# The end of a fused attention and SoLU kernel: one unit's store placed earlier, and the last unit's output split over two PSUM banks in another way

## The chip, the core and the metric

The kernel runs on one core of a Trainium2 chip. TensorE (PE) multiplies matrices into PSUM, whose eight banks hold 512 float32 numbers in each of 128 partitions. VectorE (DVE), ScalarE (ACT) and GpSimd (POOL) work on tiles, and SyncE (SP) issues most of the DMA transfers. Each engine takes its own instructions in order; engines wait for each other through semaphores. The metric is the device time of one execution in microseconds (us).

## The reference

There are two stages. The first is a linear attention with a decaying state, for 4 batches, 8 heads, 768 steps and a head size of 48. The second takes the rows of the first (3,072 rows of 384) through a layer with a SoLU activation and a layer norm:

```python
for t in range(S):
    cur = np.einsum('bhd,bhe->bhde', u[None] * kt, vt)
    y[:, :, t] = np.einsum('bhd,bhde->bhe', rt, state + cur)
    state = wt[:, :, :, None] * state + np.einsum('bhd,bhe->bhde', kt, vt)
...
h = x @ w_in
e = np.exp(h - h_max)
sm = e / (np.sum(e, axis=-1, keepdims=True) + 1e-09)
solu = h * sm
ln = (solu - mu) / np.sqrt(var + 1e-06) * g_ln
return (ln @ w_out).astype(np.float32)
```

## The kernel before

The rows are cut into 24 units of 128 rows, numbered 0 to 23 (six chunks of 128 steps, each for four batches). A unit goes through the attention and then through the second stage. Only the second stage of the last four units, 20 to 23, concerns us here.

**The second stage of a unit.** `H` multiplies the transposed rows by `w_in` into PSUM, 1,024 hidden numbers for each of 128 rows. `e` is the exponential of these (ACT), `he` the product of both (DVE), `hq` the square of `he` (ACT, in one half of the last unit DVE). `Oa` and `Ob` are the two halves of the output product (PE): `he` times `w_out`, 384 columns, and in further columns the sums that the norm needs, made with `he`, `e` (or `ea`, pairs of `e` that POOL has added) and `hq`. `w_out` carries the gain and is centred beforehand, so that the mean needs no subtraction, and the norm comes to one factor for each row. That factor takes three small steps: `qm` (DVE, the variance from the sums), `lv` (ACT, logarithm), `rs` (ACT, the inverse root through the exponential). `o` multiplies the 384 columns by it (ACT, or DVE where the word ends in `.d`), and `out` stores 192 KB to memory.

Two variants matter. Units 16, 18 and 20 turn `he` by a DMA and take their sums from other instructions; their `qm` needs a step `sq` (ACT), which reads the output's sum. The last unit, 23, is cut in halves of 512 hidden numbers: `HA`, `EA`, `DA`, `QA` are product, exponential, `he` and `hq` of the first half, `HB`, `EB`, `DB`, `QB` those of the second.

**What sets the order.** The order is written out by hand, as a long string of words, `ORDER` (lines 21 to 65). A word is a step and a unit: `qm21` is the variance of unit 21, `H22.0` the hidden product of unit 22 into bank 0. The words are carried out from first to last, and class `InOrder` (line 70) keeps the instructions of each engine in that order. So moving a word moves its instruction ahead of others on its own engine and on no other. The part of the order that the change touches is lines 62 to 64:

```python
out18 HB23.4 e22 Ob20 o19.d EA23 he22 hq22.a EB23 qm21 sq20 DA23 ea22.p lv21 qm20 lv20 DB23 QB23.d rs21 Oa22.7
QA23.a rs20 out17 Ob22 qm22 o20.a out19 lv22 Oa23.6 o21.d rs22 Ob23.s34 out20 out21 o22.a qm23 lv23 rs23 out22
o23.a out23.h
```

Ahead of these stand `H22.0` and `Oa21.2 HA23.3 Ob21`, so PE makes the hidden product of unit 22, then the first half of the output of unit 21, the first half of the hidden product of unit 23, the second half of the output of unit 21, and then `HB23` and `Ob20`.

**The output of the last unit** is made by `last_output` (line 586). It has three regions in three banks: 256 columns in bank 6, the sums (three columns) in bank 3, 128 columns in bank 4. In its first half it makes two of the eight matmuls of the 256 columns and half of the sums; in its second half the other sums, the remaining six matmuls of the 256 columns, and eight of the 128 columns. `scaled_out` (line 665) scales the 256 columns on ACT and the 128 columns on DVE, and `store` (line 676) sends the first from ACT's queue and the second from SP's.

Of the kernel before, what the change touches and what calls it, by code (L numbers as in the profile page):

```python
# [8 lines left out]
F32 = mybir.dt.float32  # L9
# [5 lines left out]
COPY = mybir.ActivationFunctionType.Copy  # L15
ALU = mybir.AluOpType
MULT, ADD, SUB = ALU.mult, ALU.add, ALU.subtract
# [41 lines left out]
e20 st19 xt19 he20 H19.0 Y22.n5 Oa17.7 kt23 e19 dv23 qm16 Ob17 y22.d ht18 M23.4 xt21 he19 lv16 rs16 o16.d Oa18.3  # L59
Ob18 hq20.a H21.0 hq18.a hq19.a m23.d ht20 xt22 out14 sq18 sv20 qm18 e21 lv18 ea19.p Y23.n2 rs18 Oa19.6 qm17  # L60
ea21.p lv17 rs17 y23.d Ob19 he21 Oa20.5 hq21.a qm19 out16 H22.0 o17.d xt23 lv19 o18.d rs19 Oa21.2 HA23.3 Ob21
out18 HB23.4 e22 Ob20 o19.d EA23 he22 hq22.a EB23 qm21 sq20 DA23 ea22.p lv21 qm20 lv20 DB23 QB23.d rs21 Oa22.7
QA23.a rs20 out17 Ob22 qm22 o20.a out19 lv22 Oa23.6 o21.d rs22 Ob23.s34 out20 out21 o22.a qm23 lv23 rs23 out22
o23.a out23.h
"""

# [34 lines left out]
def kernel(  # L101
# [14 lines left out]
    C = 128  # L116
    NC = S // C
    DM = H * D
# [3 lines left out]
    KF = DF // 128  # L122
# [4 lines left out]
    NU = len(units)  # L127

    InOrder.transfer = None
    pe, act, dve, pool, sp = (InOrder(tc, e, e in (nc.scalar, nc.sync))  # L130
                              for e in (nc.tensor, nc.scalar, nc.vector, nc.gpsimd, nc.sync))
# [13 lines left out]
    def bank(shape, dtype, slot, name):  # L145
        size = 1
        for d in shape[1:]:
            size *= d
        first = int(slot) * 512
        if dtype == BF16:  # L150
            part = banks[:, first:first + size // 2].bitcast(BF16)
        else:
            part = banks[:, first:first + size]
        if len(shape) == 2:
            return part
        names = "abc"[:len(shape) - 1]
        return part.rearrange(f"p ({' '.join(names)}) -> p {' '.join(names)}", **dict(zip(names, shape[1:])))
# [35 lines left out]
    one_col = consts.tile([C, 2], BF16)  # L193
    dve.memset(one_col, 1.0)
    inv_col = consts.tile([C, 2], BF16)
# [13 lines left out]
    w2 = consts.tile([128, KF, DM + 2], BF16)  # L209
# [126 lines left out]
    live = [dict() for _ in units]  # L336
# [245 lines left out]
    ending = [word[2:].partition(".s") for word in ORDER.split() if word.startswith(f"Ob{NU - 1}.s")]  # L582
    split = bool(ending)
    DL = DM * 2 // 3

    def last_output(i, part):
        L = live[i]
        e, he, hq = e_t[i % NWK], he_t[i % NWK], hq_t[i % NWK]
        half = range(part * KF // 2, (part + 1) * KF // 2)
        first = 2  # L590
        if part == 0:
            for f in range(first):
                pe.matmul(L["o_ps"], lhsT=he[:, f, :], rhs=w2[:, f, :DL], start=(f == 0), stop=False)
            L["s_ps"] = bank([C, 3], F32, ending[0][2][0], "s_ps")
        s_ps = L["s_ps"]
        for f in half:
            pe.matmul(s_ps[:, :2], lhsT=he[:, f, :], rhs=w2[:, f, DM:], start=(f == 0), stop=False,
                      skip_group_check=True)
            pe.matmul(s_ps[:, :2], lhsT=e[:, f, :], rhs=inv_col, start=False, stop=False, skip_group_check=True)
        for f in half:  # L600
            pe.matmul(s_ps[:, 2:], lhsT=hq[:, f, :], rhs=one_col[:, :1], start=False, stop=(f == KF - 1),
                      skip_group_check=True)
        if part:
            for f in range(first, KF):
                pe.matmul(L["o_ps"], lhsT=he[:, f, :], rhs=w2[:, f, :DL], start=False, stop=(f == KF - 1))
            r_ps = L["r_ps"] = bank([C, DM - DL], F32, ending[0][2][1], "r_ps")
            for f in range(KF):
                pe.matmul(r_ps, lhsT=he[:, f, :], rhs=w2[:, f, DL:DM], start=(f == 0), stop=(f == KF - 1))

    def output(i, part):  # L610
        L = live[i]
        e, he, hq, o_ps = e_t[i % NWK], he_t[i % NWK], hq_t[i % NWK], L["o_ps"]
        if i == NU - 1 and split:
            last_output(i, part)
            return
        for f in range(part * KF // 2, (part + 1) * KF // 2):
            if i in by_rows:
                pe.matmul(o_ps[:, :DM + 1], lhsT=he[:, f, :], rhs=w2[:, f, :DM + 1], start=(f == 0), stop=(f == KF - 1))
                continue
            pe.matmul(o_ps[:, :DM + 2], lhsT=he[:, f, :], rhs=w2[:, f, :], start=(f == 0), stop=False,  # L620
                      skip_group_check=True)
            if i not in added:
                pe.matmul(o_ps[:, DM:DM + 2], lhsT=e[:, f, :], rhs=inv_col, start=False, stop=False,
                          skip_group_check=True)
            elif f % 2 == 0:
                pe.matmul(o_ps[:, DM:DM + 2], lhsT=ea_t[i % NWK][:, f // 2, :], rhs=inv_col, start=False, stop=False,
                          skip_group_check=True)
            if i not in paired:
                pe.matmul(o_ps[:, DM + 2:], lhsT=hq[:, f, :], rhs=one_col[:, :1], start=False, stop=(f == KF - 1),
                          skip_group_check=True)  # L630
            elif f % 2 == 0:
                pe.matmul(o_ps[:, DM + 2:], lhsT=hq[:, f // 2, :], rhs=one_col[:, :1], start=False,
                          stop=(f == KF - 2), skip_group_check=True)

    def output_a(i, x):
        live[i]["o_ps"] = bank([C, DL if i == NU - 1 and split else DM + 3], F32, x, "o_ps")
        output(i, 0)

    def output_b(i, x):
# [8 lines left out]
    def variance(i, x):  # L648
        if i in by_rows:
            dve.tensor_sub(out=qm_t[i % NWK], in0=s2_t[i % NWK], in1=sq_t[i % NWK][:, 0:1])  # L650
            return
        s_ps = live[i]["s_ps"] if i == NU - 1 and split else live[i]["o_ps"][:, DM:]
        dve.tensor_scalar(out=qm_t[i % NWK], in0=s_ps[:, :1], scalar1=s_ps[:, 1:2], scalar2=s_ps[:, 2:],
                          op0=MULT, op1=ADD)

# [9 lines left out]
    def scaled_out(i, x):  # L665
        o_ps, rs, o = live[i]["o_ps"], rs_t[i % NWK], o_t[i % NWK]
        if i == NU - 1 and split:
            act.activation(out=o[:, :DL], in_=o_ps, func=COPY, scale=rs)
            dve.tensor_scalar(out=o[:, DL:], in0=live[i]["r_ps"], scalar1=rs, scalar2=None, op0=MULT)
            return  # L670
        if x == "d":
            dve.tensor_scalar(out=o, in0=o_ps[:, :DM], scalar1=rs, scalar2=None, op0=MULT)
        else:
            act.activation(out=o, in_=o_ps[:, :DM], func=COPY, scale=rs)

    def store(i, x):
# [13 lines left out]
        krk=transposed_k, krr=transposed_r, kr=transposed_copy, M=scores, m=scores_copy, sel=scores_mask,  # L690
        Y=attend, y=y_copy, S=state, et=state_decay, st=state_update, X=x_transposed, xT=x_copy,
        H=hidden, e=hidden_exp, he=hidden_mul, ea=hidden_add, qa=square_add, hq=hidden_square, Oa=output_a, Ob=output_b,
        sq=sums, qm=variance, lv=scale, rs=root, o=scaled_out, out=store,
        HA=first_half[0], EA=first_half[1], DA=first_half[2], QA=first_half[3],
        HB=second_half[0], EB=second_half[1], DB=second_half[2], QB=second_half[3],
# [36 lines left out]
```

## Time and profile before

| | |
|---|---|
| runs | 142.66, 143.30 and 144.29 us |
| median | 143.3 us |
| profiled execution: its own time | 144.28 us |
| its span, first to last instruction | 142.5 us |
| granted clock of PE, mean | 0.992 |
| PE busy | 126.0 us (88% of the span) |
| DVE busy | 122.7 us (86%) |
| ACT busy | 118.6 us (83%) |
| POOL busy | 118.4 us (83%) |

The profiled execution lies at the upper end of the three runs; 1.8 us of its time lie outside the span. In a row of the timeline the first number is the start of an instruction in microseconds from the start of the span, the second how long it took; then come the engine (PEld is PE's weight load; a q behind the name is the engine's sequencer, which issues DMAs), the line, the operation and its output and input tiles with their shapes. A bracket gives the idle time of the engine ahead of the instruction, and what ended it. All instructions go through a helper, so that all have line 86, and they are told apart by tile and shape. PSUM is the tile `ps`, `w` as an input of a matmul with `he` is the output weight.

### The profile page before, as it was taken

The page shows a single profiled execution, that of the slowest core. Times are in us where ns is not written, and L with a number is a line of the kernel's source. Part 1 is how long each engine was busy: PE and PEld are TensorE (multiplying, and loading weights), DVE is VectorE, ACT ScalarE, POOL GpSimd, SP SyncE. Part 2 cuts the span into 40 slices and gives each one's busy share as a digit, 9 for nine tenths or more (in the row PEclk, how much of TensorE's full clock was granted, in tenths as well). Part 3 has the DMA queues.
Part 4 walks back from the last instruction along what each step waited for, and adds up shares of the span by engine and source line. Part 5 has one row for each costly group of instructions (what it writes and reads, how often), then busy time and mean ns, then how long its engine had stood idle before and what let it go on. Part 6 is the DMA issues. An engine that isn't in the chain of part 4 may idle for free.

```text
span 142.5 us, 4827 instructions
## 1 busy us (share of the span) xinstructions
PE 126.0 (88%) x1901; PEld 95.7 (67%) x1906; DVE 122.7 (86%) x203; ACT 118.6 (83%) x243; POOL 118.4 (83%) x152
## 2 busy tenths in 40 slices
PE   0598966968999999999969999999999999999970
PEld 0146545657967887669858797788866766787760
DVE  6147889996999999999987999899999999878760
ACT  3658799959999999999986989998677889897780
POOL 7999999979999999999999999999999693402300
PEclk9999999999999999999999999999999999999996
DMA  4999999999999999999999899999999897562314
GB/s 93 272 300 346 316 282 384 389 293 225 249 249 244 290 250 294 246 224 230 234 191 278 197 230 212 281 158 223 176 218 208 134 246 80 136 182 68 127 59 167
DMA packets 94713, 31.98 MB, mean 224 GB/s; under 512 B 88585, under 2 KB 92818, under 8 KB 94690
## 3 DMA queue, kind: packets, MB, share of 16 engines
q1 hardware_dynamic: 70578, 20.79, 67.9%
q10 hardware_dynamic: 22128, 4.79, 15.6%
q0 software_dynamic: 1984, 6.10, 14.1%
q8 instruction: 15, 0.25, 0.7%
q14 instruction: 8, 0.07, 0.1%
HBM read 22.03 MB, written 4.72 MB: 188 GB/s over the span
## 4 chain that ended last, share of the span: by engine, by line
PE 48%; DMA 16%; POOL 14%; ACT 10%; DVE 5%; issue 3%; ACTq 0%; POOLq 0%; DVEq 0%
PE ps L86 48%; DMA win_f<-in_moe_w_in_dram 5%; DMA kr<-kp 5%; DMA kr_in<-in_r_dram 4%; POOL w L86 3%; DMA xT<-y 3%; POOL q L86 2%; ACT ps L86 2%; ACT hq L86 2%; POOL win_sb L86 1%; POOL p L86 1%; ACT e L86 1%; DVE kr L86 1%; POOL dv L86 1%; DVE he L86 1%
## 5 line engine op out<-in xcount | busy, mean ns | idle before, releaser
L86 PE MATMUL ps<-w,he 128*128 128x386 bf16 (+4 forms) x208 | 43.5, 312 | 0.0
L86 PE MATMUL ps<-xT,win_sb 128*128 128x128 bf16 x504 | 31.2, 219 | 0.2 <-DVE kr L86 0.2
L86 ACT ACTIVATE e<-ps 128x1024 bf16<-128x1024 f32 (+1 forms) x25 | 24.6, 987 | 7.5 <-PE ps L86 6.6
L86 PEld LDWEIGHTS <-win_sb 128*128 128x128 bf16 x504 | 29.0, 98 | 1.8 <-DVE kr L86 0.3
L86 DVE TENSOR_TENSOR kp<-ps,kr_in 128x768 bf16<-128x768 f32 x24 | 22.6, 950 | 7.9 <-DMA kr_in<-in_r_dram 4.2
L86 DVE TENSOR_TENSOR he<-ps,e 128x1024 bf16<-128x1024 f32 (+1 forms) x22 | 25.6, 1170 | 2.2 <-ACT e L86 1.9
L86 DVE TENSOR_TENSOR m<-ps,keep 128x1024 bf16<-128x1024 f32 x22 | 26.6, 1215 | 0.8 <-PE ps L86 0.7
L86 PE MATMUL ps<-one_col,hq 128*128 128x1 bf16 x168 | 26.7, 164 | 0.0
L86 POOL TENSOR_TENSOR p<-kr_in 128x384 bf16<-128x384 f32 x24 | 23.9, 1003 | 0.3
L86 ACT ACTIVATE hq<-he 128x1024 bf16<-128x1024 bf16 (+1 forms) x21 | 21.6, 1031 | 0.7 <-DVE he L86 0.7
L86 POOL TENSOR_TENSOR dv<-vb,dg 128x384 bf16<-128x384 bf16 x24 | 19.8, 829 | 2.6 <-DVE dg L86 2.3
L86 POOL TENSOR_TENSOR q<-p,u_bc 128x384 bf16<-128x384 bf16 x24 | 21.7, 914 | 0.1
L86 PEld LDWEIGHTS <-he 128*128 128x128 bf16 x208 | 19.1, 96 | 3.5
L86 ACT ACTIVATE ps<-ps 128x768 f32<-128x768 f32 x24 | 19.0, 796 | 2.4 <-PE ps L86 2.2
L86 PEld LDWEIGHTS <-hq 128*128 128x128 bf16 x168 | 14.1, 96 | 8.3
L86 POOL TENSOR_TENSOR ea<-e 128x512 bf16<-128x512 bf16 x9 | 10.3, 1150 | 9.4 <-ACT e L86 9.4
L86 ACT ACTIVATE lw<-w_in 128x384 bf16<-128x384 f32 x24 | 12.3, 521 | 5.5 <-DMA w_in<-in_w_dram 5.5
L86 PE MATMUL ps<-inv_col,e 128*128 128x2 bf16 x96 | 15.1, 165 | 0.0
L86 PEld LDWEIGHTS <-kp 128*128 128x128 bf16 x176 | 12.2, 104 | 3.9 <-DVE kp L86 2.1
L86 PEld LDWEIGHTS <-kr 64*128 64x128 bf16 (+1 forms) x272 | 10.3, 96 | 6.1 <-issue 1.8
L86 DVE TENSOR_REDUCE dg<-q 128x8 f32<-128x384 bf16 x24 | 12.8, 542 | 0.0
L86 POOL DMA_DIRECT2D kr_in<-in_r_dram x12 | 11.0, 921 | 0.3 <-POOL p L86 0.3
(97 smaller groups left out, 271.5 us busy)
## 6 DMA issues: line engine op xcount, KB each, us to landing
out_dram<-o SPq DMA_DIRECT2D x23, 192.0 KB, 3.2
kr_in<-in_k_dram SPq DMA_DIRECT2D x13, 192.0 KB, 5.1
kr_in<-in_r_dram POOLq DMA_DIRECT2D x12, 192.0 KB, 5.1
w_in<-in_w_dram SPq DMA_DIRECT2D x11, 192.0 KB, 5.2
kr_in<-in_r_dram SPq DMA_DIRECT2D x10, 192.0 KB, 5.3
v_in<-in_v_dram SPq DMA_DIRECT2D x10, 192.0 KB, 5.5
v_in<-in_v_dram POOLq DMA_DIRECT2D x9, 192.0 KB, 4.2
w_in<-in_w_dram ACTq DMA_DIRECT2D x8, 192.0 KB, 3.6
```

Of the source, the lines that this page charges most:

```text
L86: made = make(*args, **kwargs)
```

## The change

It has two parts.

First, in the order, `qm21 lv21 rs21` move ahead of `EA23 he22`. `o21.d` moves to a place behind `DA23`. `out17`, `out19` and `out21` move ahead of `ea22.p`; among the transfers this puts `out21` ahead of `out20`, the others keep their places. On DVE the order becomes `o19, qm21, he22, DA23, o21, qm20, DB23, QB23, qm22, qm23, o23`, where it was `o19, he22, qm21, DA23, qm20, DB23, QB23, qm22, o21, qm23, o23`. On ACT it becomes `e22, lv21, rs21, EA23, hq22, EB23, sq20, lv20, QA23, rs20, o20, ...`, where it was `e22, EA23, hq22, EB23, sq20, lv21, lv20, rs21, QA23, rs20, o20, ...`. On PE and POOL no word moves.

Second, the last unit's output has two regions: 128 columns and the three sums in bank 6, and 256 columns in bank 3. The 128 columns and two of the sums are made by one matmul of 130 columns for each of the eight parts of `he`. The 256 columns come last, in eight matmuls. There are 32 matmuls where there were 40. `scaled_out` issues the DVE instruction (128 columns) ahead of the ACT instruction (256 columns).

```diff
-out18 HB23.4 e22 Ob20 o19.d EA23 he22 hq22.a EB23 qm21 sq20 DA23 ea22.p lv21 qm20 lv20 DB23 QB23.d rs21 Oa22.7
-QA23.a rs20 out17 Ob22 qm22 o20.a out19 lv22 Oa23.6 o21.d rs22 Ob23.s34 out20 out21 o22.a qm23 lv23 rs23 out22
+out18 HB23.4 e22 Ob20 o19.d qm21 lv21 rs21 EA23 he22 hq22.a EB23 sq20 DA23 out17 out19 o21.d out21 ea22.p qm20
+lv20 DB23 QB23.d Oa22.7 QA23.a rs20 Ob22 qm22 o20.a lv22 Oa23.6 rs22 Ob23.s3 out20 o22.a qm23 lv23 rs23 out22
 o23.a out23.h
...
     def last_output(i, part):
-        half = range(part * KF // 2, (part + 1) * KF // 2)
-        first = 2
-        if part == 0:
-            for f in range(first):
-                pe.matmul(L["o_ps"], lhsT=he[:, f, :], rhs=w2[:, f, :DL], start=(f == 0), stop=False)
-            L["s_ps"] = bank([C, 3], F32, ending[0][2][0], "s_ps")
-        s_ps = L["s_ps"]
-        for f in half:
-            pe.matmul(s_ps[:, :2], lhsT=he[:, f, :], rhs=w2[:, f, DM:], start=(f == 0), stop=False,
+        for f in range(part * KF // 2, (part + 1) * KF // 2):
+            pe.matmul(L["o_ps"][:, :DM - DL + 2], lhsT=he[:, f, :], rhs=w2[:, f, DL:], start=(f == 0), stop=False,
                       skip_group_check=True)
-            pe.matmul(s_ps[:, :2], lhsT=e[:, f, :], rhs=inv_col, start=False, stop=False, skip_group_check=True)
-        for f in half:
-            pe.matmul(s_ps[:, 2:], lhsT=hq[:, f, :], rhs=one_col[:, :1], start=False, stop=(f == KF - 1),
+            pe.matmul(L["o_ps"][:, DM - DL:DM - DL + 2], lhsT=e[:, f, :], rhs=inv_col, start=False, stop=False,
                       skip_group_check=True)
+        for f in range(part * KF // 2, (part + 1) * KF // 2):
+            pe.matmul(L["o_ps"][:, DM - DL + 2:], lhsT=hq[:, f, :], rhs=one_col[:, :1], start=False,
+                      stop=(f == KF - 1), skip_group_check=True)
         if part:
-            for f in range(first, KF):
-                pe.matmul(L["o_ps"], lhsT=he[:, f, :], rhs=w2[:, f, :DL], start=False, stop=(f == KF - 1))
-            r_ps = L["r_ps"] = bank([C, DM - DL], F32, ending[0][2][1], "r_ps")
+            l_ps = L["l_ps"] = bank([C, DL], F32, ending[0][2], "l_ps")
             for f in range(KF):
-                pe.matmul(r_ps, lhsT=he[:, f, :], rhs=w2[:, f, DL:DM], start=(f == 0), stop=(f == KF - 1))
+                pe.matmul(l_ps, lhsT=he[:, f, :], rhs=w2[:, f, :DL], start=(f == 0), stop=(f == KF - 1))
...
         if i == NU - 1 and split:
-            act.activation(out=o[:, :DL], in_=o_ps, func=COPY, scale=rs)
-            dve.tensor_scalar(out=o[:, DL:], in0=live[i]["r_ps"], scalar1=rs, scalar2=None, op0=MULT)
+            dve.tensor_scalar(out=o[:, DL:], in0=o_ps[:, :DM - DL], scalar1=rs, scalar2=None, op0=MULT)
+            act.activation(out=o[:, :DL], in_=live[i]["l_ps"], func=COPY, scale=rs)
             return
```

Here `DM` is 384, `DL` is 256 and `KF` is 8.

More of the change, by code (lines that the diff above doesn't have):

```diff
@@ L635, in output_a @@
     def output_a(i, x):
-        live[i]["o_ps"] = bank([C, DL if i == NU - 1 and split else DM + 3], F32, x, "o_ps")
+        live[i]["o_ps"] = bank([C, DM - DL + 3 if i == NU - 1 and split else DM + 3], F32, x, "o_ps")
         output(i, 0)
@@ L651, in variance @@
             return
-        s_ps = live[i]["s_ps"] if i == NU - 1 and split else live[i]["o_ps"][:, DM:]
+        s_ps = live[i]["o_ps"][:, -3:]
         dve.tensor_scalar(out=qm_t[i % NWK], in0=s_ps[:, :1], scalar1=s_ps[:, 1:2], scalar2=s_ps[:, 2:],
```

## The prediction

> **What bounds the kernel now.** I read the page first, then the chain of waits in order of time, then the timeline of each engine over the last 13 us, because the first word that the change moves belongs to unit 21.
>
> ```profile
> span 142.5 us, 4827 instructions
> PE 48%; DMA 16%; POOL 14%; ACT 10%; DVE 5%; issue 3%; ACTq 0%; POOLq 0%; DVEq 0%
> ```
>
> Over the whole span the chain is mostly PE, but the change works only on the end. There the chain leaves PE:
>
> ```profile
> 120.36 10.55 PE ps L86 x156
> 130.91 0.02 issue
> 130.93 1.03 ACT e L86
> ```
>
> From 130.9 on it goes through e22 on ACT, then he22 on DVE (the first row below), and then mostly along ACT. So a step put ahead of he22 on DVE is put straight into the chain, unless its data is there by 131.98. DVE's timeline:
>
> ```profile
> 131.98 1.23 DVE L86 TENSOR_TENSOR he<-ps,e 128x1024 bf16<-128x1024 f32 x1 [0.62 <-ACT e L86]
> 133.19 0.29 DVE L86 TENSOR_SCALAR qm<-ps 128x1 f32<-128x1 f32 x1
> 133.40 0.68 DVE L86 TENSOR_TENSOR he<-ps,e 128x512 bf16<-128x512 f32 x1
> 134.88 0.16 DVE L86 TENSOR_TENSOR qm<-s,sq 128x1 f32<-128x1 f32 x1 [0.80 <-ACT sq L86]
> 134.96 0.68 DVE L86 TENSOR_TENSOR he<-ps,e 128x512 bf16<-128x512 f32 x1
> 135.67 0.69 DVE L86 SCALAR_TENSOR_TENSOR hq<-he 128x512 bf16<-128x512 bf16 x1
> 136.28 0.28 DVE L86 TENSOR_SCALAR qm<-ps 128x1 f32<-128x1 f32 x1
> 136.48 0.61 DVE L86 TENSOR_SCALAR o<-ps,rs 128x384 f32<-128x384 f32 x1
> 137.01 0.28 DVE L86 TENSOR_SCALAR qm<-ps 128x1 f32<-128x1 f32 x1
> 138.13 0.35 DVE L86 TENSOR_SCALAR o<-ps,rs 128x128 f32<-128x128 f32 x1 [0.85 <-ACT rs L86]
> ```
>
> In order these are he22, qm21, DA23, qm20, DB23, QB23, qm22, o21, qm23 and o23. PE, where qm21's data comes from and where the last unit ends:
>
> ```profile
> 132.99 0.16 PE L86 MATMUL ps<-one_col,hq 128*128 128x1 bf16 x1
> 133.01 0.83 PE L86 MATMUL ps<-xT,win_sb 128*128 128x128 bf16 x12
> ...
> 136.67 0.24 PE L86 MATMUL ps<-one_col,hq 128*128 128x1 bf16 x4
> 136.77 1.27 PE L86 MATMUL ps<-w,he 128*128 128x256 bf16 x14
> ```
>
> The first row is the last matmul of Ob21 (HB23 follows it), the last two end the sums of unit 23 and its columns. ACT:
>
> ```profile
> 133.24 1.06 ACT L86 ACTIVATE hq<-he 128x1024 bf16<-128x1024 bf16 x1 [0.19 <-DVE he L86]
> 134.21 0.58 ACT L86 ACTIVATE e<-ps 128x512 bf16<-128x512 f32 x1
> ...
> 135.07 0.29 ACT L86 ACTIVATE lv<-sq,qm 128x1 f32<-128x1 f32 x1
> 135.27 0.19 ACT L86 ACTIVATE rs<-lv 128x1 f32<-128x1 f32 x1
> 135.37 0.61 ACT L86 ACTIVATE hq<-he 128x512 bf16<-128x512 bf16 x1
> 135.88 0.19 ACT L86 ACTIVATE rs<-lv 128x1 f32<-128x1 f32 x1
> 136.10 0.58 ACT L86 ACTIVATE o<-ps,rs 128x384 f32<-128x384 f32 x1
> 136.60 0.20 ACT L86 ACTIVATE lv<-qm 128x1 f32<-128x1 f32 x1
> ...
> 137.77 0.20 ACT L86 ACTIVATE rs<-lv 128x1 f32<-128x1 f32 x1
> 138.00 0.47 ACT L86 ACTIVATE o<-ps,rs 128x256 f32<-128x256 f32 x1
> 138.51 0.37 ACTq L86 DMA_DIRECT2D out_dram<-o  x1
> ```
>
> From hq22 (133.24) to the last store's issue (138.51) ACT has hardly a gap. What is late at its start is late at its end.
>
> **The change part by part.** *qm21 ahead of he22.* Nothing ahead of Ob21 changes on PE, so the sums of unit 21 end at 132.99 + 0.16 = 133.15, 1.17 after he22 could start. On DVE he22 is now queued behind qm21, and qm21 waits. It starts between 133.15 and 133.19 (where it started before, directly behind he22). The instruction behind it followed 0.21 later (133.19 to 133.40), so he22 starts at 133.36 to 133.40 for 131.98: 1.38 to 1.42 late. I take 1.42.
>
> On ACT lv21 is queued ahead of EA23 and waits for qm21 as well, until 133.5. With rs21 that makes two steps of about 0.2, and EA23 (as long as EB23, 0.58) then ends near 134.5. The next instruction, hq22, waits for he22 until 134.66 anyway (133.24 + 1.42). So the hold on EA23 costs nothing beside the hold on he22; without that cover it would cost 1.4.
>
> *How the 1.42 travels.* hq22 134.66, EB23 135.63, qm20 (which waits for sq20 behind EB23) 136.30, lv20 136.49. rs21 no longer stands between lv20 and QA23, which saves the 0.10 between the rows at 135.27 and 135.37: QA23 136.69, rs20 137.20, o20 137.42. On DVE, qm20 at 136.30 leads as before to DB23 136.38, QB23 137.09 and qm22 137.70, and qm22 ends at 137.98. lv22 waits for that, so it starts at 138.02, again 1.42 late, and the 0.10 is lost. Then rs23 139.19, o23 on ACT 139.42, its store 139.93.
>
> *o21 and out21 earlier.* o21 (0.61) leaves its place behind qm22 for one ahead of qm20, where DVE idled 0.80 for sq20: free both before and after. Its store can go near 135.9 for 137.13, one store less in the last burst. On SP it now stands ahead of out20, whose data comes at 138.0 (136.10 + 0.58 + 1.32), so it holds nothing; `ea22.p`, which the stores are moved past, is POOL's, and POOL's order stays.
>
> *The new split.* Every input of PE is at most 1.42 late. Matmuls of 128 columns follow each other in (0.83 - 0.17)/12 = 0.055 us, so the eight of 130 columns in place of eight of 2 add at most 8 x 0.055 = 0.44 ahead of the sums' end, and the two of 256 that leave that stretch take back 0.22. The sums end by 136.91 + 1.42 + 0.22 = 138.55, qm23 by about 138.9; lv23 wants it at 138.97 (0.22 ahead of rs23). The 256 columns, 8 x 0.11 = 0.88 more, are done by about 139.4, when ACT's o23 can start. So by this upper bound PE just stays out of the way, and its saving (eight matmuls of 128 columns, at most 0.44) lies beside ACT's chain. One thing is gained: o23 on DVE started at 138.13, held by PE (whose last row ends at 138.04), though rs23 was done at 137.97; now it follows rs23 at once.
>
> *The stores.*
>
> ```profile
> 136.71 0.33 SPq L86 DMA_DIRECT2D out_dram<-o  x1
> 137.13 1.50 SPq L86 DMA_DIRECT2D out_dram<-o  x1
> 139.21 0.40 SPq L86 DMA_DIRECT2D out_dram<-o  x1
> DMA to landing us min/median/max: 1.8/2.0/3.0
> q8 instruction: 1, 0.02, 13.3%
> ```
>
> These are single rows of five answers: the issues of out20, out21 and SP's part of out23 in short windows of SP's timeline, the landing times of the stores after 124, and the instruction queue within 137.0 to 137.5. SP's last store was ready at 138.13 + 0.35 = 138.48 but issued at 139.21, because out21's issue took 1.50 in place of 0.3 to 0.4 and held SP. Now DVE's o23 ends at 139.42 + 0.35 = 139.77, and SP is free if no issue is held: 139.81, 0.60 later than before. With 2.0 to land, 141.8 (ACT's 139.93 gives 141.9), against 141.2. So between 0.6 and 0.7 of the 1.42 reach the end of this execution: 144.28 + 0.65 = 144.9.
>
> The long issue stands beside a fetch of 16 KB that took 13.3% of 16 x 0.5 us, or 1.06 us of one DMA engine. The Trainium skill ("Runtime: NRT & Kernel Launch", Instruction fetch mechanics) says that a sequencer fetches its next 16 KiB block while it executes the current one, and that this is mostly hidden. By that rule the long issue is no regular part of the kernel, and its relief no gain of the change; by the row, it would be.
>
> How this stands to the median: 143.3 is 0.98 below the profiled execution. Without the long issue out22 would have gone near 137.7 and the last store at 138.52, 0.69 sooner, which leaves the profiled execution at 143.6. So the median looks like an execution without it, and there the change costs 139.81 - 138.52 = 1.29. The ends for the median are +0.6 and +1.4; I take +1.2, near the latter: 144.5.
>
> **The rivals.** *Not slower: the stores set the end, and the wait is short.* From the last result (138.48) to the end of the span 4.0 us pass. With the shortest landing (1.8), an issue at once and the 1.3 from the last landing (141.2) to the end, they could be 3.1, so a tail without held stores gives back 0.9 at most. The wait would have to be below that: Ob21 would have to end by 132.6. If qm21 found its data by 131.98, the 0.10 on ACT and the 0.16 on DVE's o23 would come off, and up to 0.7 of tail: 142.6 to 143.2. For it: SP's held store. Against it: PE has no gap from H22 to the row at 132.99. Chance 0.10. That the new order makes no difference at all (143.3): 0.04.
>
> *A held issue again.* If a fetch meets the last stores once more, out22 (ready at 139.1) is held 1.5 and SP's part of out23 goes at 140.7, 0.9 later than in my sum: 145.4. For it: that the row exists; against it: the median. Chance 0.10.
>
> *PE's clock falls in the stall.* PE now waits for hq22, at most 1.42 longer than before.
>
> ```profile
> 139.50:140.00 0.50, 0.00 (x0) 0.00 (x0) 0.00 (x0) 0.00 (x0) 0.00 (x0) 1.00 1.05 375
> 140.00:140.50 0.50, 0.00 (x0) 0.00 (x0) 0.00 (x0) 0.00 (x0) 0.00 (x0) 0.56 1.08 398
> ```
>
> The seventh number after the stretch's length, the one ahead of the DMA share, is the granted clock. PE's last matmul ended at 138.04, and until 140.0, 1.96 later, the clock was still 1.00; it fell after that. The stall is shorter, so the clock should hold. If it fell all the same, the 3.7 us of PE work from hq22's end (134.30) to 138.04 would take 3.7/0.56 = 6.6, 2.9 more, almost all of it on the end: about 147. The Trainium skill ("TensorE: Matmul & The Clock Gate", A second HAM failure mode) tells of a kernel whose clock swung because PE idled briefly and often between groups; by that rule this would happen here, but PE's clock of 1.00 after 1.96 us of rest speaks against it. Chance 0.02.
>
> **How the numbers follow.** The forecast, that he22's wait moves the chain by 1.42 and the stores give a part of it back, has 0.74, with a time of 144.5. The held issue has 0.10 (145.4), the clock 0.02 (147), the short wait with the stores 0.10 (142.6 to 143.2), no difference 0.04 (143.3). The three runs of before lie 1.6 apart, so a median of few runs can be 0.5 off; I add that to the forecast's own ends (143.9 to 144.7), and a little of the held issue's side. The range is 143.4 to 145.4, which leaves out the clock, part of the short wait and the upper end of a held issue.
>
> One per cent is 1.4 us, about what a measurement of this kernel can tell from no change. Slower by over 1% means above 144.7: a good third of the forecast (0.28), the held issue and the clock, 0.40 together. Faster by over 1% means below 141.9, under every time that I worked out; for the short wait with a lucky median I leave 0.03. Within 1% is the rest, 0.57.
>
> **What would show it.** In the profile of the changed kernel DVE's qm21 should start near 133.2 after an idle time of about 1.8, which its row gives to PE, with he22 behind it near 133.4. hq22 should start near 134.7, ACT's o23 near 139.4, and ACT should idle about 1.5 ahead of lv21. PE should have an idle time near 135 and be done before ACT's o23. DVE's o23 should start with rs23's end, no longer with PE's. SP's issues should run o21, o20, o22, o23, with the last near 139.8 and none above 0.5.
>
> The prediction is wrong if Ob21's sums come well ahead of 133.1, so that he22 starts near 132; if the last store of SP goes at 139.2 or sooner; or if something late in the chain proves to have slack, so that ACT's o23 starts less than 1.2 later while he22 started 1.4 later.

## The result, and the profile after

The changed kernel takes 144.76 us (median of four runs, 144.43 to 145.50), the kernel before beside it 143.55 us (142.66 to 144.29). The ratio is 1.0108, with a 95% interval of 1.0064 to 1.0152: 1.2 us slower. The profiled execution of the changed kernel took 145.50 us, its span 143.8 us, for 144.28 and 142.5 us before. All ratios are of fast runs alone; the profiles of four of the kernels below (the changed one with Ob21 ahead of HA23, the kernel before with 40 more instructions, the split with 60 more, the changed one with 48 more) are of slow executions, in which PE's granted clock stood at 1.00 from e22 to the end of PE's work.

DVE's timeline of the changed kernel, from o19 on, the rows that answer to those shown of before:

```profile
131.20 0.62 DVE L86 TENSOR_SCALAR o<-ps,rs 128x384 f32<-128x384 f32 x1 [0.20 <-ACT rs L86]
133.66 0.28 DVE L86 TENSOR_SCALAR qm<-ps 128x1 f32<-128x1 f32 x1 [1.84 <-PE ps L86]
133.87 1.81 DVE L86 TENSOR_TENSOR he<-ps,e 128x1024 bf16<-128x1024 f32 x2
135.59 0.60 DVE L86 TENSOR_SCALAR o<-ps,rs 128x384 f32<-128x384 f32 x1
136.75 0.16 DVE L86 TENSOR_TENSOR qm<-s,sq 128x1 f32<-128x1 f32 x1 [0.55 <-ACT sq L86]
...
138.15 0.28 DVE L86 TENSOR_SCALAR qm<-ps 128x1 f32<-128x1 f32 x1
138.69 0.29 DVE L86 TENSOR_SCALAR qm<-ps 128x1 f32<-128x1 f32 x1 [0.26 <-PE ps L86]
139.88 0.35 DVE L86 TENSOR_SCALAR o<-ps,rs 128x128 f32<-128x128 f32 x1 [0.90 <-ACT rs L86]
```

The second row is the new wait: DVE stands idle for 1.84 us until PE ends unit 21's sums, and only then goes on with he22 (the third row, merged with DA23). ACT shows the same wait ahead of lv21, and hq22 behind both:

```profile
131.40 1.02 ACT L86 ACTIVATE e<-ps 128x1024 bf16<-128x1024 f32 x1 [0.22 <-PE ps L86]
133.98 0.20 ACT L86 ACTIVATE lv<-qm 128x1 f32<-128x1 f32 x1 [1.56 <-DVE qm L86]
134.22 0.20 ACT L86 ACTIVATE rs<-lv 128x1 f32<-128x1 f32 x1
134.32 0.58 ACT L86 ACTIVATE e<-ps 128x512 bf16<-128x512 f32 x1
135.11 1.06 ACT L86 ACTIVATE hq<-he 128x1024 bf16<-128x1024 bf16 x1 [0.21 <-DVE he L86]
...
139.87 0.47 ACT L86 ACTIVATE o<-ps,rs 128x256 f32<-128x256 f32 x1
140.38 0.36 ACTq L86 DMA_DIRECT2D out_dram<-o  x1
```

On PE the first part of Oa22 has to wait for he22 and hq22, and the last eight matmuls are over well before ACT's o23:

```profile
136.22 0.18 PE L86 MATMUL ps<-one_col,hq 128*128 128x1 bf16 x1 [0.75 <-ACT hq L86]
...
138.51 1.03 PE L86 MATMUL ps<-w,he 128*128 128x256 bf16 x8
```

SP's issues from short windows of its timeline (out20, out22, its part of out23), and the instruction queue within 138.5 to 139.5:

```profile
138.49 0.33 SPq L86 DMA_DIRECT2D out_dram<-o  x1
139.54 0.89 SPq L86 DMA_DIRECT2D out_dram<-o  x1
140.53 0.38 SPq L86 DMA_DIRECT2D out_dram<-o  x1
q8 instruction: 1, 0.02, 7.0%
```

A 16 KB fetch stands beside a long issue again, this time that of out22 (0.89 us).

The two executions differ ahead of the change too: e22 starts at 131.40, before at 130.93. PE's granted clock (the sixth number after a stretch's length, the counts in brackets left out) fell early in the profile of the changed kernel, the first pair of rows, and not in that of the kernel before, the second pair:

```profile
20.00:25.00 5.00, 3.32 (x45) 2.59 (x42) 4.82 (x8) 5.00 (x11) 4.98 (x7) 0.80 1.10 358
25.00:30.00 5.00, 5.00 (x83) 3.73 (x81) 4.87 (x6) 4.12 (x10) 4.71 (x6) 0.86 1.13 362
```

```profile
20.00:25.00 5.00, 2.98 (x54) 2.43 (x53) 5.00 (x8) 5.00 (x10) 4.98 (x7) 1.00 1.10 362
25.00:30.00 5.00, 4.83 (x86) 3.29 (x83) 5.00 (x7) 5.00 (x14) 4.71 (x6) 1.00 1.12 361
```

But the 0.47 us does not come from this fall. At 50.7 us the two executions run level again, as one step on ACT shows, first in the changed kernel, then in the one before:

```profile
50.66 0.20 ACT L86 ACTIVATE lv<-qm 128x1 f32<-128x1 f32 x1
```

```profile
50.67 0.20 ACT L86 ACTIVATE lv<-qm 128x1 f32<-128x1 f32 x1
```

Behind that each of them has PE wait for a transposing transfer, the kernel before for 1.2 us (for `kr`, between 72 and 78), the changed one for 1.4 us (for `xT`, between 79 and 88), and between 103 and 109 the changed one falls back by another 0.2. Why these waits differ isn't shown. The change touches nothing there.

So all that follows counts from the start of e22 on ACT, the last point that neither the change nor an experiment on the end touches. Times in the table are microseconds after it, from one profiled execution each. "Held" is the longest issue of a store on SP, with its unit; "fetch" is the start of the last 16 KB fetch.

| kernel | e22 at | he22 | ACT's o23 | held | fetch | SP's last store | end of span |
|---|---|---|---|---|---|---|---|
| before | 130.93 | 1.05 | 7.07 | 1.50 (21) | 6.26 | 8.28 | 11.54 |
| changed | 131.40 | 2.47 | 8.47 | 0.89 (22) | 7.54 | 9.13 | 12.38 |
| order alone | 130.67 | 2.47 | 8.49 | 0.82 (22) | 7.27 | 9.07 | 12.30 |
| split alone | 131.22 | 1.05 | 7.07 | 1.38 (21) | 6.18 | 8.15 | 11.42 |
| changed, Ob21 ahead of HA23 | 132.07 | 1.80 | 7.81 | 0.84 (22) | 6.67 | 8.41 | 11.65 |
| changed, wait on ACT | 130.11 | 1.06 | 7.68 | 1.39 (22) | 6.82 | 8.83 | 11.94 |
| before, 80 more PE instructions | 134.02 | 1.06 | 7.08 | none | 2.48 | 7.58 | 10.79 |
| before, 40 more | 132.65 | 1.05 | 7.08 | none | 4.44 | 7.58 | 10.80 |
| split, 40 more | 131.39 | 1.06 | 7.08 | none | 4.34 | 7.46 | 10.69 |
| split, 60 more | 133.44 | 1.06 | 7.08 | none | 4.37 | 7.46 | 10.66 |
| before, 48 more near the end | 130.31 | 1.06 | 7.08 | none | 4.63 | 7.64 | 10.86 |
| split, 48 more near the end | 130.08 | 1.06 | 7.08 | none | 4.71 | 7.46 | 10.67 |
| changed, 48 more near the end | 132.32 | 2.50 | 8.51 | none | 6.00 | 8.89 | 12.11 |

### The profile page after: what moved, and what is told of

Same layout as the page of the kernel before. It is cut to its first block, busy times and chain, and to the rows that moved or that the text cites. A ratio compares the mean times of both kernels' runs of the same rounds, so it can differ in the third digit from the quotient of the medians.

```text
span 143.8 us, 4811 instructions
## 1 busy us (share of the span) xinstructions
PE 127.0 (88%) x1893; PEld 96.0 (67%) x1898; DVE 122.8 (85%) x203; ACT 118.9 (83%) x243; POOL 118.4 (82%) x152
## 4 chain that ended last, share of the span: by engine, by line
PE 34%; POOL 26%; DMA 17%; ACT 8%; issue 7%; DVE 4%; ACTq 0%; POOLq 0%
PE ps L86 34%; DMA w_in<-in_w_dram 8%; DMA xT<-y 7%; POOL p L86 6%; POOL kr_in L86 6%; DVE he L86 3%; POOL dv L86 3%; POOL q L86 3%; DMA out_dram<-o 3%; ACT e L86 2%; POOL v_in L86 2%; ACT hq L86 2%; POOL m L86 1%; ACT o L86 1%; POOL w_in L86 1%
## 5 line engine op out<-in xcount | busy, mean ns | idle before, releaser
L86 PE MATMUL ps<-w,he 128*128 128x386 bf16 (+3 forms) x200 | 43.6, 318 | 0.2 <-DVE he L86 0.2
L86 PEld LDWEIGHTS <-kp 128*128 128x128 bf16 x176 | 12.7, 107 | 3.5 <-DVE kp L86 1.5
L86 DVE TENSOR_TENSOR st<-ps,et 128x384 bf16<-128x384 f32 x20 | 10.9, 547 | 0.7 <-ACT et L86 0.7
```

The source lines that it names most:

```text
L86: made = make(*args, **kwargs)
```

## The experiments

**The order alone**: the new order with the old split.

```diff
-lv20 DB23 QB23.d Oa22.7 QA23.a rs20 Ob22 qm22 o20.a lv22 Oa23.6 rs22 Ob23.s3 out20 o22.a qm23 lv23 rs23 out22
+lv20 DB23 QB23.d Oa22.7 QA23.a rs20 Ob22 qm22 o20.a lv22 Oa23.6 rs22 Ob23.s34 out20 o22.a qm23 lv23 rs23 out22
...
-        for f in range(part * KF // 2, (part + 1) * KF // 2):
-            pe.matmul(L["o_ps"][:, :DM - DL + 2], lhsT=he[:, f, :], rhs=w2[:, f, DL:], start=(f == 0), stop=False,
...
+        half = range(part * KF // 2, (part + 1) * KF // 2)
+        first = 2
```

(The rest of the second part of the change is taken back in the same way.)

> The changed order with the old split of the last unit (three regions, 40 matmuls). Theory, the wait: he22 still stands behind qm21 on DVE, so from the start of e22 on ACT to the start of ACT's o23 it takes 8.4 to 8.5 us, as in the changed kernel (8.47), for 7.07 before; the time is within 0.4 us of the changed kernel's. Rival, the new split costs the time: 7.1 us on that stretch and the time of the kernel before.

Measured: 8.49 us from e22 to ACT's o23, and a ratio to before of 1.0069 (1.0029 to 1.0109). DVE's timeline has the same wait:

```profile
132.94 0.29 DVE L86 TENSOR_SCALAR qm<-ps 128x1 f32<-128x1 f32 x1 [1.84 <-PE ps L86]
133.14 1.81 DVE L86 TENSOR_TENSOR he<-ps,e 128x1024 bf16<-128x1024 f32 x2
```

The order alone makes the kernel slower. It is 0.39% below the changed kernel's ratio, 0.6 us where 0.4 was allowed for; the two intervals overlap.

**The split alone**: the old words in the changed kernel, with one bank named for the 256 columns.

```diff
-QA23.a rs20 out17 Ob22 qm22 o20.a out19 lv22 Oa23.6 o21.d rs22 Ob23.s34 out20 out21 o22.a qm23 lv23 rs23 out22
+QA23.a rs20 out17 Ob22 qm22 o20.a out19 lv22 Oa23.6 o21.d rs22 Ob23.s3 out20 out21 o22.a qm23 lv23 rs23 out22
```

> The old order with the new split (two regions, 32 matmuls). Theory, the wait: he22 goes at once, the stretch from e22 to ACT's o23 is 7.0 to 7.1 us as before, only DVE's o23 starts 0.1 to 0.2 sooner; the time is the kernel before's, at most 0.3 us less. Rival, the split costs the time: 8.4 us on that stretch, and about 1.2 us slower than before.

Measured: 7.07 us on that stretch, DVE's o23 at 7.08 for 7.20, the end 0.12 sooner, and a ratio of 1.0012 (0.9970 to 1.0053). DVE and SP:

```profile
132.27 1.22 DVE L86 TENSOR_TENSOR he<-ps,e 128x1024 bf16<-128x1024 f32 x1 [0.63 <-ACT e L86]
```

```profile
137.42 1.38 SPq L86 DMA_DIRECT2D out_dram<-o  x1
```

The split costs nothing. The 0.12 us at the end are not the split's doing, though: SP is busy with out21 and out22 until 8.06 after e22, when DVE's o23 has been done since 7.43, and the fetch beside out21's issue ends 0.12 sooner after e22 here (7.21 for 7.33). What the split is worth shows below, where no issue is held. And out21's issue is long again: it was no accident of the first profile.

**A shorter wait**: in the changed kernel Ob21 goes ahead of HA23 on PE, so that qm21's data comes sooner.

```diff
-ea21.p lv17 rs17 y23.d Ob19 he21 Oa20.5 hq21.a qm19 out16 H22.0 o17.d xt23 lv19 o18.d rs19 Oa21.2 HA23.3 Ob21
+ea21.p lv17 rs17 y23.d Ob19 he21 Oa20.5 hq21.a qm19 out16 H22.0 o17.d xt23 lv19 o18.d rs19 Oa21.2 Ob21 HA23.3
```

> The changed kernel with HA23 moved behind Ob21 on PE, so that the sums of unit 21 end about 0.65 us sooner and nothing else moves. Theory, the wait sets the cost: he22 starts 0.65 us sooner and ACT's o23 too, 7.8 us after e22 for 8.47; the time is 0.4 to 0.7 us under the changed kernel's. Rival, the cost lies behind he22 (ACT's order, the split, the stores): the stretch stays at 8.4 us. Rival, HA23 itself becomes late: EA23 moves and hq22 with it, 8.2 us or more.

```profile
133.67 0.29 DVE L86 TENSOR_SCALAR qm<-ps 128x1 f32<-128x1 f32 x1 [1.17 <-PE ps L86]
133.87 1.86 DVE L86 TENSOR_TENSOR he<-ps,e 128x1024 bf16<-128x1024 f32 x2
```

DVE's idle time falls from 1.84 to 1.17, by 0.67, and ACT's o23 comes 0.66 sooner (7.81 for 8.47). The ratio to before is 1.0011 (0.9981 to 1.0041), against 1.0108 of the changed kernel. The chain follows the length of this wait one to one. The time itself comes 1.0%, or 1.4 us, under the changed kernel's, more than the 0.4 to 0.7 expected; the end in the profiles comes 0.73 sooner (11.65 for 12.38), and what the rest is isn't shown.

**The wait moved to ACT**: in the changed kernel EA23 and he22 go first again, while lv21 and rs21 stay ahead of hq22.

```diff
-out18 HB23.4 e22 Ob20 o19.d qm21 lv21 rs21 EA23 he22 hq22.a EB23 sq20 DA23 out17 out19 o21.d out21 ea22.p qm20
+out18 HB23.4 e22 Ob20 o19.d EA23 he22 qm21 lv21 rs21 hq22.a EB23 sq20 DA23 out17 out19 o21.d out21 ea22.p qm20
```

> The changed kernel with EA23 and he22 put back ahead of qm21, lv21 and rs21, which now stand ahead of hq22 on ACT; o21 and out21 stay early. Theory: he22 starts at once (1.05 us after e22), but hq22 is queued on ACT behind lv21, which waits for qm21, and starts 3.1 us after e22 for 2.31 before and 3.71 in the changed kernel; ACT's o23 follows 7.7 to 7.9 us after e22, and the time lies 0.5 to 0.7 under the changed kernel's. Rival, only the wait on DVE counts: 7.1 us, and the time of before.

```profile
132.70 0.20 ACT L86 ACTIVATE lv<-qm 128x1 f32<-128x1 f32 x1 [0.47 <-DVE qm L86]
132.93 0.20 ACT L86 ACTIVATE rs<-lv 128x1 f32<-128x1 f32 x1
133.04 1.04 ACT L86 ACTIVATE hq<-he 128x1024 bf16<-128x1024 bf16 x1
```

e22 starts at 130.11 here, so hq22 comes 2.93 after it (expected 3.1), and o23 7.68 after it (expected 7.7 to 7.9): the two small steps stand in the chain, 0.6 us of it. The ratio is 0.9989 (0.9959 to 1.0020). That is 1.2%, or 1.7 us, under the changed kernel's, where 0.5 to 0.7 us was expected, and better than this stretch can explain; e22 comes 0.8 sooner than in the profile of before, for which nothing in the edit is a reason.

**Moving the fetch.** 80 instructions more on PE, at its very start:

```diff
-LU0 LR3.g LW3.a LW1.a LW2.g lw3 LR0.a cum3.0 LG0 ih0 ex3 LW0 gs0.7 LK3 LR2.g hot1.2 LV0.g ik0 LK0 lw1 lw0 LV3.g
+LU0 LR3.g LW3.a pad40.2 LW1.a LW2.g lw3 LR0.a cum3.0 LG0 ih0 ex3 LW0 gs0.7 LK3 LR2.g hot1.2 LV0.g ik0 LK0 lw1 lw0 LV3.g
...
+    def padding(i, x):
+        dest = bank([128, 512], F32, x, "pad_ps")
+        for j in range(i):
+            pe.matmul(dest[:, :2], lhsT=warm[:, :128], rhs=warm[:, :2], start=True, stop=True)
```

> The kernel before with 40 matmuls of 2 columns (80 instructions on PE) put at PE's very start, where it waits for the first loads; their result is not used. Every later instruction of PE stands 80 places further on, so the last 16 KB fetch should come 2 to 3 us sooner, ahead of the last stores. Theory, the fetch holds the store: out21's issue takes 0.3 to 0.4 us for 1.50, SP's last issue comes 7.6 us after e22 for 8.28, and the end 0.5 to 0.7 us sooner. Rival, the long issue has another cause (two stores in a row): it stays above 1 us, with the fetch elsewhere.

```profile
140.22 0.38 SPq L86 DMA_DIRECT2D out_dram<-o  x1
q8 instruction: 1, 0.02, 9.1%
```

The rows are out21's issue and the instruction queue within 136.0 to 137.0, 2.5 us after e22 (134.02). The fetch starts 3.8 us sooner after e22, where 2 to 3 was expected. With it gone from the stores out21's issue takes 0.38 us, SP's last store goes at 7.58, and the end comes 10.79 after e22 for 11.54: 0.75 sooner. So the extra instructions on PE move this fetch, and the fetch is what holds the store. But the kernel is slower, 1.0170 (1.0103 to 1.0237), for e22 comes 3.1 us later. The list of waits between 97 and 107 has the place:

```profile
ACT ps L86 <- PE ps L86: 2.7, 1, 2.7
PEld L86 <- DMA kr<-kp: 2.2, 1, 2.2
```

PE waits for a transposing transfer, which it didn't before. All fetches move with the extra instructions, and one now starts at 92.80, ahead of it; that this fetch is the reason is argued, not shown.

Fewer instructions: the ten warm-up matmuls in thirds or quarters, so that PE's time for them stays.

```diff
-        for j in range(i):
-            pe.matmul(dest, lhsT=warm[:, :128], rhs=warm, start=True, stop=True)
+        cut = 3 if i == 10 else 1
+        for j in range(i * cut):
+            pe.matmul(dest[:, :512 // cut], lhsT=warm[:, :128], rhs=warm[:, :512 // cut], start=True, stop=True)
```

> The kernel before with its ten warm-up matmuls of 512 columns made as thirty of 170 (a warm-up's result is not used): PE's time for them stays, PE has 40 instructions more from there on, and each 16 KB fetch comes that much sooner. Theory, the fetch holds the last stores: the last fetch starts 0.6 to 0.8 us sooner against e22, out21's issue takes 0.4 us for 1.50, and the span ends 10.8 us after e22 for 11.54; the other fetches move too, and where one meets a transfer that PE waits for, e22 itself comes later, as with 80 instructions. Rival: 1 us or more for out21's issue in spite of the moved fetch.

> The old order, the new split of the last unit, and the warm-up in thirds (40 instructions more on PE). Theory: ACT's o23 7.07 us after e22 as with the split alone, no held store, the end 10.6 to 10.8 us after e22 for 11.54 of the kernel before and 12.38 of the changed one; if no fetch meets a transfer elsewhere, 0.5 us faster than the kernel before. Rival, the moved fetches cost in the middle what they save at the end: e22 later by 1 us or more, and slower than before.

> As the last one, with the warm-up as forty matmuls of 128 columns (60 instructions more on PE). Theory: the same end, 10.6 to 10.8 us after e22; whether e22 comes at the time of before depends on where the other fetches fall, so the two may differ in e22's time by 1 us or more and not in the end.

The end is as expected in all three (10.80, 10.69 and 10.66 after e22), and no issue is held. The fetch moved further than expected: with 40 more it starts at 4.44 for 6.26, 1.8 us sooner and not 0.6 to 0.8. The split is worth 0.11 us at the end (10.69 for 10.80), which DVE's o23 and SP's last store give it, both 0.12 sooner. The times aren't settled by it: 0.9981 (0.9939 to 1.0022) for the kernel before in thirds, 0.9977 (0.9937 to 1.0016) for the split in thirds, 1.0062 (1.0018 to 1.0107) for the split in quarters. In its profile the last one loses 1.3 us between 98 and 109, where PE waits for a transposing transfer once more; one profile doesn't show that the ratio comes from this:

```profile
PEld L86 <- DMA xT<-y: 1.4, 1, 1.4
PE ps L86 <- DMA xT<-y: 1.3, 1, 1.3
```

So the fetch had to be moved where no other one moves with it. In the next three kernels the 24 matmuls of 128 columns in HA23 and HB23 become 48 of 64. They lie behind the last fetch but one.

```diff
-                for j in range(KM):
-                    pe.matmul(h_ps[:, f, :], lhsT=win_sb[:, j, g * 128:(g + 1) * 128], rhs=xT_t[i % NWK][:, j, :],
-                              start=(j == 0), stop=(j == KM - 1))
+                for t in (slice(0, C // 2), slice(C // 2, C)):
+                    for j in range(KM):
+                        pe.matmul(h_ps[:, f, t], lhsT=win_sb[:, j, g * 128:(g + 1) * 128], rhs=xT_t[i % NWK][:, j, t],
+                                  start=(j == 0), stop=(j == KM - 1))
```

> The kernel before, with the 24 matmuls of 128 columns in HA23 and HB23 made as 48 of 64 columns: 48 instructions more on PE, all of them behind the last fetch but one, so that only the last fetch moves. Theory, the fetch holds the stores: it starts 4 to 5 us after e22 for 6.26, out21's issue takes 0.4 us, the span ends 10.8 us after e22 for 11.54, e22 comes within 0.6 us of the time of before, and the kernel is 0.5 to 0.7 us faster. Rival, the narrow matmuls cost more than half of the wide ones: PE ends later and EA23 with it, no gain.

Measured: 0.9945 (0.9912 to 0.9979), 0.8 us faster than the kernel before. The end comes 10.86 after e22, 0.68 sooner; out21's issue:

```profile
136.52 0.38 SPq L86 DMA_DIRECT2D out_dram<-o  x1
```

> The same with the new split of the last unit in the old order: the change without its new order, and the last fetch moved. Theory: 10.65 to 10.7 us from e22 to the end, 0.85 less than before, and the kernel 0.6 to 0.8 us faster than before. Rival as for the last one.

Measured: 0.9931 (0.9897 to 0.9965), 1.0 us faster than before, the end 10.67 after e22. It has the change's split, the old order and the moved fetch, and beats both kernels. The split's part of the end is 0.19 us here (10.67 for 10.86). The fetch within 134.0 to 135.0, and out21's issue:

```profile
q8 instruction: 1, 0.02, 5.5%
136.28 0.38 SPq L86 DMA_DIRECT2D out_dram<-o  x1
```

> The changed kernel with the same 48 matmuls. Theory: he22 2.47 and ACT's o23 8.48 us after e22 as in the changed kernel; the fetch is over before out22's issue, which takes 0.4 us for 0.89, and SP's last store goes at 8.9 for 9.13, so the end comes 12.0 to 12.1 us after e22 for 12.38: the chain's whole 1.4 us now shows against the last kernel (12.05 - 10.67). Rival, the stores would have hidden a part of the wait: under 11.7.

Measured: 1.0049 (1.0015 to 1.0083), the end 12.11 after e22. The wait on DVE stands as it was (he22 at 2.50, o23 at 8.51), and out22 and out23 go unhindered:

```profile
140.50 0.33 SPq L86 DMA_DIRECT2D out_dram<-o  x1
141.21 0.33 SPq L86 DMA_DIRECT2D out_dram<-o  x1
```

Between this kernel and the one ahead of it only the order differs. ACT's o23 comes 8.51 - 7.08 = 1.43 later, the end 12.11 - 10.67 = 1.44 later. From o23 to the end both take 3.60 and 3.59. So the store of unit 21 placed earlier is worth nothing by itself. It paid only where a fetch held SP: from o23 to the end the kernel before takes 11.54 - 7.07 = 4.47, the split alone 4.35 and the changed kernel 3.91, for behind the held issue two stores are left in the first two and one in the last. How much it pays varies with the fetch: with the wait on ACT, where out21 goes early too, the fetch ends late and the stretch takes 11.94 - 7.68 = 4.26.

**How the fetch holds a store.** The six profiles with a held issue agree in one more thing. The times are microseconds after e22; the fetch's end is its start and its length in the trace's record of transfers.

| kernel | fetch | held issue | from the fetch's end to the issue's |
|---|---|---|---|
| before | 6.26 to 7.33 | 6.21 to 7.71 | 0.38 |
| changed | 7.54 to 8.67 | 8.15 to 9.04 | 0.37 |
| order alone | 7.27 to 8.60 | 8.15 to 8.97 | 0.37 |
| split alone | 6.18 to 7.21 | 6.20 to 7.58 | 0.37 |
| changed, Ob21 ahead of HA23 | 6.67 to 7.95 | 7.48 to 8.32 | 0.37 |
| changed, wait on ACT | 6.82 to 8.36 | 7.34 to 8.74 | 0.37 |

The issue lasts until the fetch has ended, and then about as long as an issue of its own (0.33 to 0.41). So where the fetch's end falls sets the length of the hold, and with it when the last store can go.

## Why the prediction was right, and where it wasn't

**The wait.** Right in mechanism and size. qm21's row names PE after 1.84 us of idle time (about 1.8 was forecast), and he22 comes 1.42 later after e22 (2.47 for 1.05). The order alone carries it, the split alone does not, and a wait shorter by 0.67 gives back 0.66. The rival of a short wait fell with it: qm21 finds its data 2.26 us after e22 in both kernels.

**The hold on EA23.** Right: EA23 ends at 134.90, hq22 starts at 135.11 and waits for he22.

**How the 1.42 travels.** Right: after e22, o20 comes 6.48 for 5.17 (1.31 later), lv22 7.07 for 5.67, ACT's o23 8.47 for 7.07 (both 1.40 later). The 0.10 that rs21 leaves is lost again at qm22, as forecast.

**The new split.** Right. PE ends 139.54 - 131.40 = 8.14 after e22, 0.3 ahead of ACT's o23; the bound had it just in time. DVE's o23 starts with ACT's (139.88 and 139.87) and no longer behind PE. At the end of the span it is worth 0.11 to 0.19 us where no store is held, and nothing where one is, for there SP and not DVE's o23 sets the last store.

**PE's clock.** The rival fell. PE's pauses for he22 and hq22 are 0.17 and 0.75 us, and the granted clock in the stretch with the longer of them and the one behind it:

```profile
135.00:136.00 1.00, 0.34 (x2) 0.11 (x2) 1.00 (x3) 0.89 (x1) 0.00 (x0) 1.00 0.03 8
136.00:137.00 1.00, 0.78 (x9) 0.53 (x10) 0.45 (x3) 0.77 (x4) 0.00 (x0) 1.00 0.00 0
```

The rule of the Trainium skill ("TensorE: Matmul & The Clock Gate", A second HAM failure mode), by which the clock would have swung, does not show at this place. Two readings of the rival were off, which changes nothing in its fall: the granted clock is the sixth number of a row and not the seventh, and the 0.56 is the mean of a stretch in which it fell from 1.00 to 0.50 (from 140.1 to 140.5 the view gives 0.50), so the fall would have cost 3.7 us and not 2.9.

**The stores.** Here a size was off. The sum had SP free, its last store 0.60 later and the end 0.65 later. Out22's issue was held (0.89), the store came 9.13 - 8.28 = 0.85 later, and the end 12.38 - 11.54 = 0.84. The rival of a held issue, given 0.10, came true in this part: with 0.89 for the 1.5 that it was priced at.

**How it stands to the median.** This step failed, although the number that came of it was close: "So the median looks like an execution without it, and there the change costs 139.81 - 138.52 = 1.29." The held issue is in the profile of every kernel whose last fetch wasn't moved (0.82 to 1.50 us), and moving that fetch alone makes the kernel before 0.55% faster. A median without it would have gained nothing. The sum of 1.29 was a right one for an execution that these two kernels don't have: with the fetch moved in both, SP's last store goes 8.89 - 7.64 = 1.25 later and the end comes 12.11 - 10.86 = 1.25 later. As they stand, the end of the profile moved by 0.84, the held issue included. So it is in part luck that the +1.2 taken for the median met the measured 1.2 us. The interval of that begins at 0.64% of 143.55, or 0.9 us, and the order alone came out at 1.0 us, 0.4 to 1.6. What the rest beyond 0.84 is isn't shown, nor why the profiled execution of before took 0.98 us more than the median.

**The fetch.** The rule of the Trainium skill that a fetch is mostly hidden ("Runtime: NRT & Kernel Launch", Instruction fetch mechanics) was left as a possibility. PE itself shows no cost: its last 14 matmuls run on through the fetch (136.77 to 138.04, the fetch from 137.19). But at this place the fetch cost the kernel before 11.54 - 10.86 = 0.68 us at its end, through SP's stores.

## What to carry to other kernels

Before a step is moved ahead of another on an in-order engine, compare when the moved step's input is ready with when the overtaken step could start; the difference, here 1.4 us, goes into the chain as it stands, and the wait's row in the new profile must show it. A store issued sooner was worth something here only where the last stores waited for each other, so look first at what holds them. When a transfer's issue is long in a single place, look for an instruction fetch beside it: 40 to 80 instructions more ahead of it moved it here, best behind the last fetch but one, so that no other moved along.

## What the runs showed of the hardware

A 16 KB instruction fetch of PE, which takes 0.9 to 1.5 us of one DMA engine as the last one of a profile, lengthened a store's issue on SP to between 0.82 and 1.50 us, from between 0.33 and 0.41, in all six profiles in which it started 0.2 to 0.5 us after out20's issue, and in none of the other seven, in which it started ahead of that. In the six the issue ended 0.37 to 0.38 us after the fetch. A fetch alone does not hold an issue: a store issued at 111.66 in the profile of before, inside a fetch from 111.47 to 112.40, took 0.34, and out20's issue in the changed kernel with 48 more, 7.12 us after e22 inside a fetch from 6.00 to 7.36, took 0.33. Each of the held ones had another store's issue just ahead of the fetch; what this does in the queue isn't shown. It comes on the way through PE's instructions, not through time: 80 instructions more at the start brought it 3.8 us sooner (2.48 for 6.26 after e22). With 40, 48 and 60 instructions more in the old order it starts at nearly the same time, 4.3 to 4.7; why these don't differ isn't settled.

In six of the thirteen profiles, those of the changed kernel, of the shorter wait, of 40, 40 and 60 more instructions, and of the changed kernel with 48 more, PE's granted clock fell once between 22 and 37 us (in the changed kernel to 0.80 and 0.86 over two stretches of 5 us, which is 0.50 from 23.0 to 26.4). In these e22 starts at 131.39 to 133.44, in the six with no fall ahead of it at 130.08 to 131.22. (With 80 more instructions it fell later, between 102 and 106, right behind where PE waited for the transfer.) In five of the six ACT runs 1.3 to 1.8 us behind the kernel before at 38 us, behind the fall; in the changed kernel it runs level there, so a fall need not show later. The waits for transposing transfers behind that move e22 as well, so no time of e22 is put down to an edit here.
